# Summing the decays of both parities on TensorE for the first two token pairs, with a new order of all steps

## The chip, the cores and the metric

The kernel runs on one core of a Trainium2 chip. A core has five engines that run their own instruction streams: TensorE (PE, matrix products), VectorE (DVE), ScalarE (ACT), GpSimd (POOL) and SyncE (SP, which here only issues transfers), and sixteen DMA engines that carry transfers between the chip's memory (HBM) and the core's on-chip memory (SBUF). Matrix products end in a second on-chip memory, PSUM, with 8 banks. The metric is the device time of one execution in microseconds (us); lower is better. A median over several runs is compared.

## The reference

Two parts follow each other. The first is a linear attention with a gated state; its output is reshaped to tokens and goes through a two-layer network with the activation h * cos(h).

```python
batch, n_heads, seq, head_dim = (4, 8, 768, 48)
f = 1.0 / (1.0 + np.exp(-f_logit))
for t in range(S):
    state = f[:, :, t, :, None] * state + np.einsum('bhd,bhe->bhde', k[:, :, t], v[:, :, t])
    y[:, :, t] = np.einsum('bhd,bhde->bhe', q[:, :, t], state)
...
x = y.transpose(0, 2, 1, 3).reshape(B * S, H * D)       # 3072 x 384
h = x @ w_in                                            # 3072 x 2048
g = h * np.cos(h)
out = g @ w_out                                         # 3072 x 384
```

All inputs and the output are float32.

## The kernel before

**Tiling.** The 3072 tokens are cut into 12 *pairs* of 256 tokens (three pairs to a batch element). A pair has 128 partitions with two neighbouring tokens each, the even and the odd *parity* (`e` in the code), and in time two halves `g` of 128 tokens. All 8 heads are handled together, in two groups `u` of 4. The network works on the same 256-token units: its first layer is cut into 8 steps per unit (`h0.00` is unit 0, column quarter 0, half 0: 6 matmuls of 256 columns), its second into 8 (`o2.3` is output tile 2 of 128 tokens, quarter 3 of the hidden columns: 4 matmuls of 384 columns).

**The steps of a pair**, by name: the gate's logits, k, q and v are loaded (`f`, `k`, `q`, `v`, transfers issued on SP; pairs 0 and 1, in the list `HALVES`, load f, k and q in two halves, so `q0.1` is pair 0, heads 4 to 7). ACT makes log(1 + exp(-f)) (`ex`, `ln`). The decay over time is a running sum of this, made on PE by a product with a triangular matrix (`cum`), and ACT takes the exponential of it with both signs (`eb`, `ei`). q is multiplied by the one and k by the other (`qm`, `km`). Before, the sum is common to both parities of a partition, and the step by which they differ is put in ahead: `fx` (ACT) recovers a gate, `qa` multiplies q of the even parity, `ka` k of the even parity. q and k are turned, for pairs 0 to 3 by PE (`tq`, `tk`, copied from PSUM by `qkt`), from pair 4 on by a transposing transfer on SP (`tq`). PE makes the scores (`sc`), DVE masks them (`am`), PE multiplies them with v (`y`; v is converted by `vb` and rearranged by four `vt`), and PE adds the part of the state carried in (`yi`). The output goes to SBUF by two `xe`. The state is k times v (`ps`, PE); DVE adds the old state (`st`) and multiplies by the total decay (`sz`).

**The network**: `w0.i` and `w1.i` load the two weights in four blocks each, and `wc` converts them. After two `h` steps ACT takes the cosine (`co`) and DVE multiplies (`g`). After four `o` steps the tile is copied from PSUM (`ot`) and sent out (`out`).

**The order.** Nothing is scheduled at run time. A string, `ORDER`, lists every step with its engine's letter (T is PE, S ACT, V DVE, G POOL, Y SP) and the buffers that it takes; `emit` walks it, and each engine runs its own steps in that order, waiting by semaphores where data or a buffer is not there yet. So a step that waits holds up all that stands behind it on its engine. `SLOTS` gives the number of buffers of each kind. Steps `zf` are matmuls of zeros (`ZEROS` of them) that nothing reads; they stand on PE between the steps of the start. Steps `z..` with another name fill buffers with zeros once.

The profile names steps by line: `f`, `k`, `q`, `v` L296, `w` L282, `cum` L374 and L380, `eb` and `ei` L391 (pairs 0 and 1) and L395, `qa` L338 and L341, `ka` L351, `ad` (the sum of both parities for later pairs) L363, `qm` and `km` L404, `tq` and `tk` on PE L435 and as transfers L424, `sc` L456, `am` L461, `ps` L479, `st` L497, `sz` L503, `y` and `yi` L531, `g` L561, `h` L579, `co` L584, `o` L595, `out` L606, `zf` L264; all copies and conversions (`qkt`, `vb`, `vt`, `xe`, `ot`, `wc`) stand in one helper, L197, and are told apart by their tiles.

Of the kernel before, what the change touches and what calls it, by code (L numbers as in the profile page):

```python
# [16 lines left out]
C = 128  # L17
# [9 lines left out]
VHALVES = ()  # L27
TURN_QK = range(4, 12)
UNITS = [256] * 12
SLOTS = {"f": 3, "k": 3, "q": 3, "v": 3, "sp": 3, "ls": 2, "b": 3, "bi": 3, "qk": 3, "vb": 3, "vt": 3, "qkt": 5, "am": 4,  # L30
         "sz": 4, "x": 4, "g": 5, "co": 4, "ot": 4}
WITHIN = 12
ZEROS = 52
# [3 lines left out]
zvt.2:V zsp.2:V f0.1:Y0 zqk.2:G zsp.0:G f0.0:S ex0.1:S ln0.1:S2 f1.0:Y2 ex0.0:S fx0.1:S ln0.0:S  # L37
zf0:T0 zf1:T0 zf2:T0 zf3:T0 zf4:T0 zf5:T0 zf6:T0 zf7:T0 zf8:T0 zf9:T0 zf10:T0 cum0.0:T4 zvt.1:G
fx0.0:S zqk.0:G zsz.2:G k0.1:Y2 ka0.1:G cum0.1:T7 ei0.1:S1 km0.1:G0 eb0.0:S1 ei0.0:S ex1.0:S eb0.1:S
q0.0:Y0 v0:Y0 vb0:S0 ln1.0:S2 qa0.0:V qm0.0:V zsz.3:G zf11:T0 zf12:T0 zf13:T0 zf14:T0 zf15:T0  # L40
zf16:T0 zf17:T0 zf18:T0 zf19:T0 zf20:T0 zf21:T0 zf22:T0 zf23:T0 zf24:T0 cum1.0:T1 k0.0:Y ka0.0:G
km0.0:V zf25:T0 ps0.0:T6,7 f1.1:Y ex1.1:S ps0.1:T q0.1:Y ei1.0:S0 eb1.0:S0 ln1.1:S fx1.1:S qa0.1:V
sz0.01:V2 sz0.00:V st0.11:V f2:Y1 vt0.1:G2 zvt.0:V st0.10:V vt0.3:G qm0.1:G tk0.0:T0 tq0.0:T
qkt0.0:V0 v1:Y2 vt0.0:G ex2:S ln2:S1 k1.0:Y1 fx1.0:S zsp.1:G k1.1:Y zf26:T2 tk0.1:T6 zf27:T2 tq0.1:T
cum1.1:T3 qkt0.1:V1 zsz.1:G zsz.0:G zf28:T2 sc0.0:T4 am0.0:V2 sc0.1:T0 ad2:G0 sz0.10:V0 am0.1:V0
ei1.1:S eb1.1:S vb1:S1 vt1.2:S0 zf29:T2 zf30:T2 zf31:T2 zf32:T2 cum2:T2 ei2:S2 eb2:S2 ka1.0:V
zqk.1:G km1.0:V1 zf33:T6 zf34:T6 zf35:T6 zf36:T6 zf37:T6 zf38:T6 zf39:T6 zf40:T6 tk1.0:T4 ps1.0:T6,1
f3:Y0 ex3:S q1.0:Y1 sz0.11:V qa1.0:V q1.1:Y qa1.1:V qm1.1:V ln3:S0 fx3:S ka1.1:G vt0.2:G km1.1:G
ps1.1:T y0:T3,5 yi0:T xe0.0:S0 vt1.3:S vt1.1:S fy3:S st1.01:V st1.00:V sz1.01:V1 zf41:T0 zf42:T0
zf43:T0 tq1.1:T0 sz1.00:V qm1.0:G tq1.0:T qkt1.0:S2 tk1.1:T qkt1.1:V0 zf44:T2 zf45:T2 zf46:T2  # L50
zf47:T2 sc1.1:T6 xe0.1:V fx2:S ad3:G1 cum3:T0 ei3:S1 sc1.0:T4 am1.1:V1 am1.0:V3 w0.1:Y0 vt1.0:G
wc0.1:G zf48:T2 zf49:T2 zf50:T2 zf51:T2 h0.11:T2 h0.10:T yi1:T7,6 st1.11:V sz1.11:V3 y1:T xe1.1:V2
st1.10:V sz1.10:V eb3:S1 co0.1:S3 xe1.0:S g0.1:V3 fy2:S w0.0:Y1 wc0.0:G h0.01:T4 h0.00:T h1.01:T6
co0.0:S0 g0.0:V h1.00:T co1.0:S1 g1.0:V2 h1.10:T0 h1.11:T co1.1:S2 g1.1:V k3:Y2 ka3:G km3.1:G2
w0.3:Y4 wc0.3:G h0.31:T2 h0.30:T w0.2:Y0 wc0.2:G h1.21:T4 h1.20:T h0.20:T6 co0.3:S3 g0.3:V co1.2:S0
# [48 lines left out]
h9.00:T0 sz10.00:V1 st10.01:V sz10.01:V st10.11:V st10.10:V sz10.10:V0 sz10.11:V st11.00:V h9.01:T
co9.0:S3 st11.01:V g9.0:V1 h9.20:T4 h9.21:T h9.10:T2 co9.2:S0 sz11.01:V3 g9.2:V sz11.00:V o16.3:T6
# [83 lines left out]
def describe(nc, cpool, ppool, q, k, v, f_logit, moe_w_in, moe_w_out, out):  # L189
# [3 lines left out]
    def tl(shape, dt, name):  # L193
        return cpool.tile(shape, dt, name=name)
# [523 lines left out]
```

## Time and profile before

| | us |
|---|---|
| three runs | 180.91, 181.43, 182.29 |
| median | 181.43 |
| span of the profiled execution (first to last instruction) | 179.3 |
| median less that span | 2.13 |
| PE busy in the span | 171.0 (95%) |
| DVE, ACT, POOL busy | 137.8, 131.3, 109.2 |
| idle time of PE after 25 us, before matmuls | 1.2 |
| first `h` matmul | 25.1 |
| matmuls of zeros: 50 recorded | 14.8 |

The profiled execution is given by its span alone; the runs' times hold also what lies around a span. The profile's rows name a group by its source line, engine, operation and tiles, then count, busy time, mean of one in ns, and the idle time of the engine just before these instructions with what ended it. A time line's rows are start, duration, engine, line, operation. In the chain of waits each row is start, length and what the end was waiting for.

### The profile page before, as it was taken

The numbers are of one execution on the slowest core, as the hardware profiler recorded it, in microseconds if no ns is written. First come the engines' busy times: TensorE is split into PE (matmuls) and PEld (weight loads), VectorE is DVE, ScalarE is ACT, GpSimd is POOL, SyncE is SP. The second block draws the span as 40 slices with busy tenths as digits, with TensorE's granted clock in tenths as the row PEclk, the third lists the DMA queues.
The fourth block names the chain that finished last, engine by engine and source line by source line (L and its number), as shares of the span: only waits on it lengthen the run. The fifth ranks groups of instructions, "written<-read, shape, count | busy, mean of one in ns | idle before, by whom it ended". The sixth has DMA issues, their size and how long they took to land.

```text
span 179.3 us, 5727 instructions
## 1 busy us (share of the span) xinstructions
PE 171.0 (95%) x2412; PEld 122.9 (69%) x2414; DVE 137.8 (77%) x206; ACT 131.3 (73%) x185; POOL 109.2 (61%) x139
## 2 busy tenths in 40 slices
PE   7998899999999999999999998999999999999992
PEld 2453568876578866778668885668877766867761
DVE  6379998998894989969899887768689996385330
ACT  3899878886999998988999979858973702364410
POOL 7498699976979998789977295827992000000000
PEclk9999999999999999999999999999999999999999
DMA  6999999999999799999999999959045900004013
GB/s 156 262 261 287 356 324 315 306 274 328 257 257 236 168 190 180 282 277 198 249 203 262 226 254 207 234 131 268 4 106 121 148 0 4 4 0 176 0 50 129
DMA packets 74394, 34.46 MB, mean 192 GB/s; under 512 B 67456, under 2 KB 72832, under 8 KB 74368
## 3 DMA queue, kind: packets, MB, share of 16 engines
q1 hardware_dynamic: 73696, 33.79, 81.4%
q8 instruction: 19, 0.31, 0.8%
q10 hardware_dynamic: 672, 0.30, 0.6%
q14 instruction: 7, 0.06, 0.1%
HBM read 25.17 MB, written 4.72 MB: 167 GB/s over the span
## 4 chain that ended last, share of the span: by engine, by line
PE 69%; DMA 10%; POOL 7%; SPq 5%; DVE 5%; issue 3%; ACT 0%; POOLq 0%; DVEq 0%; ACTq 0%
PE ps L595 29%; PE ps L579 29%; DMA q<-in_q_dram 7%; SPq L296 5%; PE ps L531 4%; DMA qkt<-qk 3%; PE ps L456 3%; POOL qk L404 3%; PE ps L479 1%; POOL sp L363 1%; PE ps L435 1%; DVE qk L404 1%; POOL vt L197 1%; DVE sz L503 1%; PE ps L374 1%
## 5 line engine op out<-in xcount | busy, mean ns | idle before, releaser
L561 DVE TENSOR_TENSOR g<-ps,co 128x1024 bf16<-128x1024 f32 x48 | 57.7, 1221 | 15.3 <-ACT co L584 11.3
L595 PE MATMUL ps<-w_out_bf,g 128*128 128x384 bf16 x384 | 68.4, 326 | 0.0
L579 PE MATMUL ps<-x,w_in_bf 128*128 128x256 bf16 x576 | 66.7, 273 | 0.4 <-issue 0.4
L584 ACT ACTIVATE co<-ps,halfpi 128x1024 bf16<-128x1024 f32 x48 | 52.6, 1115 | 17.7 <-PE ps L579 14.4
L579 PEld LDWEIGHTS <-w_in_bf 128*128 128x128 bf16 x576 | 55.8, 98 | 9.2 <-issue 0.6
L595 PEld LDWEIGHTS <-g 128*128 128x128 bf16 x384 | 36.0, 98 | 21.5
L461 DVE TENSOR_TENSOR am<-ps,pmask 128x1024 bf16<-128x1024 f32 x24 | 28.7, 1215 | 3.6 <-PE ps L456 3.5
L404 POOL TENSOR_TENSOR qk<-q,b 128x384 bf16<-128x384 f32 x22 | 21.9, 1002 | 2.6 <-DVE q L338 1.7
L404 POOL TENSOR_TENSOR qk<-k,bi 128x384 bf16<-128x384 f32 x22 | 21.9, 1007 | 1.6 <-ACT bi L391 1.1
L197 POOL COPY vt<-vb 64x384 bf16<-64x384 bf16 x31 | 15.9, 514 | 1.4
L264 PE MATMUL ps<-zero 128*128 128x512 bf16 x50 | 14.8, 435 | 1.3 <-DVE zero L203 1.2
L503 DVE TENSOR_TENSOR sz<-ps,b 64x192 bf16<-64x192 f32 x40 | 14.2, 354 | 1.9 <-PE ps L479 0.9
L351 POOL TENSOR_TENSOR k<-k,f 128x384 f32<-128x384 f32 (+1 forms) x13 | 11.7, 904 | 6.2 <-DMA k<-in_k_dram 2.9
L197 DVE COPY ot<-ps 128x384 f32<-128x384 f32 (+1 forms) x17 | 8.7, 519 | 8.5 <-PE ps L595 6.0
L341 POOL TENSOR_TENSOR q<-f,q 128x384 f32<-128x384 f32 x10 | 10.0, 999 | 8.1 <-DMA q<-in_q_dram 8.1
L363 POOL TENSOR_TENSOR sp<-ls 128x384 bf16<-128x384 f32 x10 | 10.3, 1029 | 4.4 <-issue 2.2
L497 DVE TENSOR_TENSOR ps<-ps,sz 64x192 f32<-64x192 f32 x32 | 11.7, 366 | 1.4 <-PE ps L479 0.3
L329 ACT ACTIVATE f<-f 128x768 f32<-128x768 f32 (+1 forms) x14 | 10.4, 748 | 2.7 <-DMA f<-in_f_logit_dram 2.5
L197 ACT CAST x<-ps 128x384 bf16<-128x384 f32 x12 | 5.5, 479 | 8.6 <-PE ps L531 8.6
L197 ACT COPY ot<-ps 128x384 f32<-128x384 f32 (+1 forms) x9 | 4.1, 455 | 8.9 <-PE ps L595 8.9
L456 PE MATMUL ps<-qkt 48*64 48x128 bf16 (+1 forms) x320 | 8.6, 219 | 1.9 <-DVE qkt L197 1.0
L264 PEld LDWEIGHTS <-zero 128*128 128x128 bf16 x52 | 5.1, 108 | 6.9 <-issue 2.5
(61 smaller groups left out, 166.2 us busy)
## 6 DMA issues: line engine op xcount, KB each, us to landing
v<-in_v_dram SPq DMA_DIRECT2D x12, 384.0 KB, 6.1
out_dram<-ot SPq DMA_DIRECT2D x22, 192.0 KB, 2.8
f<-in_f_logit_dram SPq DMA_DIRECT2D x10, 384.0 KB, 5.6
k<-in_k_dram SPq DMA_DIRECT2D x10, 384.0 KB, 6.1
q<-in_q_dram SPq DMA_DIRECT2D x10, 384.0 KB, 6.4
g<-in_moe_w_in_dram SPq DMA_DIRECT2D x4, 768.0 KB, 7.5
g<-in_moe_w_out_dram SPq DMA_DIRECT2D x4, 768.0 KB, 7.2
k<-in_k_dram SPq DMA_DIRECT2D x4, 192.0 KB, 5.0
```

Source lines behind the costliest of these rows:

```text
L197: (nc.scalar.copy if e == "ACT" else eng(e).tensor_copy)(out=o, in_=i)
L264: G.step(f"zf{i}", ("PE",), lambda e, dump=dump: nc.tensor.matmul(dump.ap, lhsT=zero[:, 0:128], rhs=zero, start=True, stop=True), writes=[ ...
L351: eng(e).tensor_mul(out=w.ap[:, :, 0, :], in0=w.ap[:, :, 0, :], in1=t.ap[:, :, 0, :])
L363: G.step(f"ad{n}", ("POOL",), lambda e: eng(e).tensor_add(out=sp.ap[:, 0, :, 0:D], in0=soft.ap[:, :, 0, :], in1=soft.ap[:, :, 1, :]), read ...
L404: G.step(f"{nm}{n}.{u}", ("POOL", "DVE") if cut else ("POOL",), lambda e, u=u, j=j, src=src, dec=dec: eng(e).tensor_mul(out=qkp[u][j].ap[: ...
L456: nc.tensor.matmul(o[t0:t1, r, 2 * a + g, :].rearrange("p (e n) -> p e n", e=2), lhsT=wide[s, t0 // 64, :] if turned else wide[s].rearrang ...
L461: G.step(f"am{n}.{u}", ("DVE",), lambda e, u=u, sc=sc: nc.vector.tensor_mul(out=am[u].ap.rearrange("p r b n -> p (r b) n"), in0=sc.ap.rear ...
L503: eng(e).tensor_mul(out=new.ap[s, :, r, :].rearrange("p (u a) n -> p u a n", u=2), in0=view()[s].rearrange("p (u a) n -> p u a n", u=2), i ...
L561: nc.vector.tensor_mul(out=o.rearrange("p b (n e) -> p b n e", e=2), in0=ph.ap.rearrange("p (b e n) -> p b n e", e=2, n=64), in1=co.ap.rea ...
L579: nc.tensor.matmul(ph.ap[:, i * T:(i + 1) * T].rearrange("p (g t) -> p g t", t=C), lhsT=w_in_bf[:, kk, f0:f0 + 128], rhs=xa[:, :, kk, :], ...
L584: G.step(f"co{m}.{j}", ("ACT",), lambda e, ph=ph, co=co: nc.scalar.activation(out=co.ap, in_=ph.ap, func=AF.Sin, bias=halfpi), reads=[ph], ...
L595: nc.tensor.matmul(po.ap[:, 0:DM], lhsT=gT.ap[:, j, i * C:(i + 1) * C], rhs=w_out_bf[:, j, :], start=(po.first and j == 4 * s), stop=(po.f ...
```

## The change

For pairs 0 and 1 the running sum is now made for each parity by itself. `cum` does four matmuls of 192 columns for a half in the place of two: for the odd parity's contribution to the even one it takes the strict triangle. So the steps `fx`, `qa` and `ka` of these pairs are left out, and `eb` and `ei` are twice as wide (388 and 384 columns for 196 and 192) into new buffers `bb`, `bj`. For pair 1 (`CARRY_PE`) the old state is no longer added by DVE: `si` multiplies it with the identity on PE and sums it into the same PSUM bank. There are 33 matmuls of zeros for 52. `VLIE` and what belongs to it is empty and adds no instruction. The order of all steps is new.

```diff
-ZEROS = 52
+VLIE = ()
+CARRY_PE = (1,)
+ZEROS = 33
...
         pcs = [Val(p1), Val(p1)] if cut else [Val(p1)]
         xe = (0, 1) if cut else (0,)
+        W = HB * len(xe)
 
         def cum(e, o, h0, hn):
...
-            for x in xe:
-                nc.tensor.matmul(o[:, :, 0:HB], lhsT=incl,
-                                 rhs=w[:, x, :, 0:D].rearrange("p (u h) d -> p u h d", u=un),
-                                 start=(x == 0), stop=False)
+            for z in xe:
+                for x in xe:
+                    nc.tensor.matmul(o[:, :, HB * z:HB * z + HB], lhsT=strict if x > z and cut else incl,
+                                     rhs=w[:, x, :, 0:D].rearrange("p (u h) d -> p u h d", u=un),
+                                     start=(z == 0 and x == 0), stop=False)
...
-        for nm, dst, dh, sc, w in (("eb", bt, bth, -1.0, HB + 4), ("ei", bi, bih, 1.0, HB)):
+        for nm, dst, dh, sc, w in (("eb", bt, bth, -1.0, W + 4), ("ei", bi, bih, 1.0, W)):
...
             G.step(f"ln{n}{u}", ("ACT",), lambda e, t=t, s=s: ln(e, t, s), reads=[t], writes=[s], table="E")
+            if cut:
+                continue
...
-            if S0 is not None:
+            if S0 is not None and n in CARRY_PE:
+                def add(e, g=g, S0=S0):
+                    for r in range(2):
+                        nc.tensor.matmul(ps[g].ap[:, 0:HB].rearrange("p (a n) -> p a n", n=D), lhsT=ident,
+                                         rhs=S0.ap[:, :, r, :], start=(ps[g].first and r == 0),
+                                         stop=(ps[g].final and r == 1))
+                G.step(f"si{n}.{g}", ("PE",), add, reads=[S0] + both, writes=[ps[g]], sums=True)
+            elif S0 is not None:
...
-zvt.2:V zsp.2:V f0.1:Y0 zqk.2:G zsp.0:G f0.0:S ex0.1:S ln0.1:S2 f1.0:Y2 ex0.0:S fx0.1:S ln0.0:S
+f0.0:Y1 zf0:T7 f0.1:Y zf1:T2 f1.1:Y2 zsz.0:G v0:Y0 k0.1:Y0 k1.0:Y1 ex0.0:S q0.1:Y0 zsp.2:V zsz.2:V
```

The first place is the start of the program. SP's queue of loads before (f, k, q and v are the inputs, the number behind a name is the buffer):

```order
L296 DMA f_94<-in_f_logit_dram 128x4x96
L296 DMA f_96<-in_f_logit_dram 128x4x96
L296 DMA k_99<-in_k_dram 128x4x96
L296 DMA q_100<-in_q_dram 128x4x96
L296 DMA v_103<-in_v_dram 128x8x96
L296 DMA k_99<-in_k_dram 128x4x96
L296 DMA f_96<-in_f_logit_dram 128x4x96
L296 DMA q_100<-in_q_dram 128x4x96
```

And now:

```order
L309 DMA f_96<-in_f_logit_dram 128x4x96 x2
L309 DMA f_97<-in_f_logit_dram 128x4x96
L309 DMA v_104<-in_v_dram 128x8x96
L309 DMA k_98<-in_k_dram 128x4x96
L309 DMA k_99<-in_k_dram 128x4x96
L309 DMA q_101<-in_q_dram 128x4x96
L309 DMA f_97<-in_f_logit_dram 128x4x96
L309 DMA k_98<-in_k_dram 128x4x96
L309 DMA q_103<-in_q_dram 128x4x96
L309 DMA q_101<-in_q_dram 128x4x96
```

One more half of f, which ACT issued before, is in SP's queue, and the last row, `q0.0`, moved from the fourth place of SP's queue to the eleventh; halves of pair 1 (`k_99`, `f_97`, `q_103`) went ahead of it.

DVE in the same stretch before, from the masks of pair 0's scores (`am`) on; `k` and `q` rows are `ka` and `qa`, `qk` rows `km` and `qm`, `ps<-ps,sz` is `st`:

```order
L461 TENSOR_TENSOR am_131<-ps_158,pmask 128x1024
L351 TENSOR_TENSOR k_98<-k_98,f_96 128x4x48
L404 TENSOR_TENSOR qk_118<-k_98,bi_114 128x8x48
L503 TENSOR_TENSOR sz_135<-ps_161,b_112 64x4x48
L338 SCALAR_TENSOR_TENSOR q_101<-f_96,q_101 128x4x48 x2
L404 TENSOR_TENSOR qk_118<-q_101,b_111 128x8x48
L497 TENSOR_TENSOR ps_161<-ps_161,sz_135 64x192 x2
L503 TENSOR_TENSOR sz_136<-ps_161,b_111 64x4x48 x2
```

And now, from the same `am` on:

```order
L494 TENSOR_TENSOR am_137<-ps_165,pmask 128x1024
L544 TENSOR_TENSOR sz_141<-ps_166,bb_124 64x4x48 x2
L196 CAST x_147<-ps_166 128x384
L544 TENSOR_TENSOR sz_143<-ps_164,bb_124 64x4x48
L196 COPY qkt_133<-ps_163 128x1024
```

Between the masks of pair 0 and the state of pair 1, DVE has lost the preparation of k and q and the additions of the old state.

POOL in the same stretch now, from `vb1` to the first converted weight block (`wc0.1`) and the two `vt` steps behind it:

```order
L196 CAST vb_122<-v_105 128x768
L416 TENSOR_TENSOR qk_120<-k_99,bj_126 128x8x48
L416 TENSOR_TENSOR qk_120<-q_103,bb_124 128x8x48
L416 TENSOR_TENSOR qk_120<-k_99,bj_126 128x8x48
L196 COPY vt_130<-vb_121 64x8x48
L241 MEMSET sz_141 128x384
L373 TENSOR_TENSOR sp_108<-ls_110 128x8x48
L241 MEMSET qk_118 128x32x16
L416 TENSOR_TENSOR qk_120<-q_103,bb_124 128x8x48
L373 TENSOR_TENSOR sp_109<-ls_110 128x8x48
L196 CAST w_in_bf<-g_151 128x3x512
L196 COPY vt_128<-vb_122 64x8x48 x2
```

All four multiplies of pair 1 stand on POOL here, with the conversion of its v; before, POOL had two of the four.

The second place is the end of the program on ACT, the last copies and outputs, before:

```order
L584 ACTIVATE co_151<-ps_161,halfpi 128x1024
L197 COPY ot_154<-ps_158 128x384
L197 COPY ot_155<-ps_158 128x384
L197 COPY ot_152<-ps_160 128x192
L606 DMA out_dram<-ot_152 128x192
```

And now:

```order
L639 ACTIVATE co_153<-ps_164,halfpi 128x1024
L196 COPY ot_158<-ps_166 128x192
L661 DMA out_dram<-ot_158 128x192 x2
L661 DMA out_dram<-ot_159 128x192
L196 COPY ot_159<-ps_166 128x192
L661 DMA out_dram<-ot_159 128x192
L196 COPY ot_160<-ps_165 128x384
L196 COPY ot_158<-ps_165 128x384
```

The halved tiles 22 and 23 are no longer the last: the last two copies are whole tiles (20 and 21), and SP sends them; four issues of halves moved to ACT's queue.

More of the change, by code (lines that the diff above doesn't have):

```diff
@@ L38 @@
[L38 to L55, printed above, removed]
@@ new lines @@
+zf15:T6 zsp.1:G tk0.0:T5 ei1.1:S0 zf16:T4 qm0.0:V q1.1:Y tq0.0:T cum1.0:T6 qkt0.0:S0 w0.1:Y3
+ps0.0:T0,7 vb1:G1 zf17:T1 zf18:T1 ei1.0:S ps0.1:T zf19:T3 eb1.0:S sz0.00:V0 w0.0:Y1 km1.0:G2
+sz0.01:V zf20:T6 ex2:S zf21:T6 st0.11:V zf22:T5 qm1.0:G qkt0.1:V1 sc0.0:T0 ln2:S0 ps1.0:T6,3
+sz0.11:V2 sc0.1:T4 km1.1:G zf23:T2 st0.10:V vt1.1:S0 zf24:T2 am0.0:V2 zf25:T2 w0.2:Y2 fx2:S zf26:T2
+vt0.0:G tq1.0:T2 vt1.3:S ps1.1:T zsz.1:G sz0.10:V zf27:T0 ad2:G1 am0.1:V1 tk1.0:T si1.0:T k3:Y1
+zf28:T1 ex3:S zf29:T0 zqk.0:G zf30:T0 yi0:T7 sz1.01:V1 qm1.1:G ln3:S0 y0:T5 sz1.00:V si1.1:T
```

229 lines of the change are left out of this document (140 added, 89 removed).

## The prediction

> **What bounds the kernel now.** I read the page's first table first.
>
> ```profile
> PE 171.0 (95%) x2412; PEld 122.9 (69%) x2414; DVE 137.8 (77%) x206; ACT 131.3 (73%) x185; POOL 109.2 (61%) x139
> ```
>
> TensorE (PE) is the engine to follow, but 95% is an average over stages with different limits. So I took the groups of PE from 25 us to the end, with the idle time before them, and then the chain of waits.
>
> ```profile
> L579 PE MATMUL ps<-x,w_in_bf 128*128 128x256 bf16 x576 | 66.7, 273 | 0.4 <-issue 0.4
> L456 PE MATMUL ps<-qkt 48*64 48x128 bf16 (+1 forms) x288 | 7.0, 219 | 0.8 <-DMA qkt<-qk 0.6 <-ACT bi L395 0.2
> ```
>
> After 25 us PE is idle for 1.2 us in all (0.4 + 0.8). Time can come only from three places: the start before the first real MoE matmul, that 1.2 us, and the tail. The chain of waits shows start and end (start us, us, what):
>
> ```profile
> 6.01 4.53 DMA q<-in_q_dram
> ...
> 16.84 1.08 DVE k L351
> ...
> 19.66 1.17 DVE qk L404
> ...
> 25.08 1.31 PE ps L579 x12
> 26.39 0.90 PE ps L531 x56
> 27.29 2.73 PE ps L579 x24
> ...
> 168.21 7.81 PE ps L595 x48
> ```
>
> The start hangs on a load of q until 10.5 us and then on VectorE (DVE), which prepares pairs 0 and 1. First `h` at 25.08; two `h` steps and pair 1's output are done at 27.29; from there PE is packed to 168.21 + 7.81 = 176.02. The span is 179.3 us, the median of the runs 181.43, so 2.13 us lie outside the span; I add changes to that median.
>
> **Start.** The change takes off DVE, for pairs 0 and 1, four `qa`, one `ka`, two `km` and the four `st` of pair 1:
>
> ```profile
> L338 DVE SCALAR_TENSOR_TENSOR q<-f,q 128x192 f32<-128x192 f32 x4 | 1.4, 363 | 2.6 <-DMA q<-in_q_dram 2.6
> L497 DVE TENSOR_TENSOR ps<-ps,sz 64x192 f32<-64x192 f32 x32 | 11.7, 366 | 1.4 <-PE ps L479 0.3
> ```
>
> 4 x 0.363 + 4 x 0.366 + the 1.08 us of `ka` in the chain are 4.0 us even without `km`, so the old DVE chain is gone. What is late next? First the loads. Rows of POOL and DVE that waited for loads:
>
> ```profile
> 6.01 0.59 POOL L351 TENSOR_TENSOR k<-k,f 128x192 f32<-128x192 f32 x1 [2.07 <-DMA k<-in_k_dram]
> 10.56 0.38 DVE L338 SCALAR_TENSOR_TENSOR q<-f,q 128x192 f32<-128x192 f32 x1 [0.20 <-DMA q<-in_q_dram]
> ```
>
> In units of a 192 KB half load, k0.1 was the 4th on the queues and q0.1 the 10th: 6 units in 4.55 us, 0.76 us each. In the new order q0.0 is the 12th unit (it was the 5th): 6.01 + 8 x 0.76 = 12.1 us. The first w_in block is unit 21 to 24 in both: about 21.2 us. That `f0.0` moves from ACT's queue to the head of SyncE's (SP) I cost at nothing: ACT's first work waits for the data, and the count starts with the same three f halves. Now the pieces behind q0.0 (groups: busy, mean ns; then one row of PE's time line):
>
> ```profile
> L404 DVE TENSOR_TENSOR qk<-q,b 128x384 bf16<-128x384 f32 x2 | 2.5, 1234 | 0.7 <-ACT b L391 0.6
> L197 ACT COPY qkt<-ps 128x1024 bf16<-128x1024 bf16 x2 | 2.0, 1002 | 0.5 <-PE ps L435 0.5
> L395 ACT ACTIVATE bi<-ps 128x384 f32<-128x384 f32 x10 | 4.7, 489 | 1.5 <-PE ps L380 1.5
> L461 DVE TENSOR_TENSOR am<-ps,pmask 128x1024 bf16<-128x1024 f32 x24 | 28.7, 1215 | 3.6 <-PE ps L456 3.5
> 12.50 0.39 PE L435 MATMUL ps<-ident,qk 128*128 128x128 bf16 x4
> ```
>
> `qm0.0` on DVE ends at 12.1 + 1.23 = 13.3, `tq0.0` on PE at 13.7, `qkt0.0` on ScalarE (ACT) at 14.7. `cum1.0` is queued on PE behind `tq0.0` and hides under that copy: the nearest row is the transposes' 0.39 us for four matmuls, and eight give 0.8; if it took over 1.0, the rest would shift by the excess. `ei1.0`, now as wide as the L395 row, ends at 15.2 and releases GpSimd (POOL). POOL then has, without a gap: `km1.0`, `qm1.0`, `km1.1`, `vt0.0`, a memset, `ad2`, a memset, `qm1.1`, `ad3`, `wc0.1`, and `vt1.2`, `vt1.0`, `wc0.0`.
>
> ```profile
> L404 POOL TENSOR_TENSOR qk<-k,bi 128x384 bf16<-128x384 f32 x22 | 21.9, 1007 | 1.6 <-ACT bi L391 1.1
> L404 POOL TENSOR_TENSOR qk<-q,b 128x384 bf16<-128x384 f32 x22 | 21.9, 1002 | 2.6 <-DVE q L338 1.7
> L363 POOL TENSOR_TENSOR sp<-ls 128x384 bf16<-128x384 f32 x10 | 10.3, 1029 | 4.4 <-issue 2.2
> L197 POOL COPY vt<-vb 64x384 bf16<-64x384 bf16 x31 | 15.9, 514 | 1.4
> L197 POOL CAST w_in_bf<-g 128x1536 bf16<-128x1536 f32 x4 | 5.8, 1464 | 0.3 <-DMA g<-in_moe_w_in_dram 0.3
> L231 POOL MEMSET sz<- 128x384 bf16 x4 | 1.6, 421 | 0.0
> L231 POOL MEMSET qk<- 128x512 bf16 x3 | 1.6, 540 | 0.0
> ```
>
> To the end of `wc0.1`: 3.02 + 0.51 + 0.42 + 1.03 + 0.54 + 1.00 + 1.03 + 1.46 = 9.0, so 24.2 us; then 1.03 + 1.46, so `wc0.0` ends at 26.7. DVE arrives together with it: `qm1.1` ends on POOL at 21.7, its transposes (0.4), one state product before and one after, and the copy bring DVE to about 23.6, and two `am` (2 x 1.215) to 26.1; `y1` follows by 26.6. So PE stands at 26.7 where it stood at 27.29: 0.6 us gained. Of ACT's removed `fx` and its wider `eb` and `ei` only `qkt0.0` and `ei1.0` stand on this path, and they are in the sum. The wait added is that of the two `si` steps for pair 0's state: queued behind `si1.0` on PE are `yi0` and `y0`, and `y0` waits longer anyway, for `am0.1` on DVE. I cost `si` at nothing; without that cover each is two 192-column matmuls, together under 0.4 us by the transposes' row. Bounds: the best start has `wc0.1` right behind its load, 21.2 + 1.46 = 22.7 for the first `h` against 25.08, a gain of 2.4; the worst stretches POOL as in these rows of the two engines:
>
> ```profile
> 16.53 1.17 POOL L404 TENSOR_TENSOR qk<-k,bi 128x384 bf16<-128x384 f32 x1
> 20.38 1.31 POOL L363 TENSOR_TENSOR sp<-ls 128x384 bf16<-128x384 f32 x1
> 16.76 1.15 DVE L351 TENSOR_TENSOR k<-k,f 128x192 f32<-128x192 f32 x1
> ```
>
> 1.17 against 1.007 and 1.31 against 1.029, 16 to 27% on 11.5 us, 1.8 to 3.1 us lost, so at worst 2.5 slower. I take the undisturbed means, since both long POOL rows lie beside DVE instructions that read two SBUF tiles (the L351 row, and the L404 row at 19.66 in the chain), and in the new order DVE has none of these after 13.3 us. [...]
>
> **Fillers.** 52 become 33. One, `zf32`, now stands behind the first `h`:
>
> ```profile
> 1.19 4.88 PE L264 MATMUL ps<-zero 128*128 128x512 bf16 x11 [1.19 <-DVE zero L203]
> 7.09 3.21 PE L264 MATMUL ps<-zero 128*128 128x512 bf16 x14
> ```
>
> It costs 3.21 / 14 = 0.23 us. The others lay before 25.08 where PE waited anyway.
>
> **Middle.** The same `h`, `o` and attention steps in another order: no PE work more or less. I keep 1.2 us of stalls; bounds 0 (a gain of 1.2) and the rival below.
>
> **Tail.** The last two outputs now are whole 192 KB tiles: `ot21` on ACT, `out21` on SyncE's queue. Before, it was two half copies and halves of 96 KB.
>
> ```profile
> 176.79 0.35 ACTq L606 DMA_DIRECT2D out_dram<-ot  x1
> L197 ACT COPY ot<-ps 128x384 f32<-128x384 f32 (+1 forms) x9 | 4.1, 455 | 8.9 <-PE ps L595 8.9
> out_dram<-ot SPq DMA_DIRECT2D x7, 192.0 KB, 2.1
> out_dram<-ot ACTq DMA_DIRECT2D x1, 96.0 KB, 1.6
> v<-in_v_dram SPq DMA_DIRECT2D x12, 384.0 KB, 6.1
> ```
>
> Before: 0.77 + 1.6 = 2.37 us from the last matmul to landing. Now 0.05 + 0.46 + 0.03 + 2.1 = 2.64: 0.3 us more. Ahead of the two copies ACT now has two half copies and four output issues, four times 0.35 by the first row: counted from the end of `o22.2`, 3.25 us before the end, they take 2 x 0.46 + 4 x 0.35 = 2.3 us and are through 0.3 us before tile 20's last matmul; without that cover the tail grows by what is over. Bounds: 0 if ACT is at hand at once, and 1 us if `out20`, issued 0.65 us earlier, delays it (twice the size in one queue; the v row, 6.1 us among other loads, is the far bound and no neighbour here).
>
> Sum: -0.6 + 0.23 + 0 + 0.3 = -0.1, so 181.3 us. 1% (1.8 us) is about what measurement can tell from no change.
>
> **Rivals.** *Faster*: the loads land sooner than by count, POOL starts early, and the start wins its bound of 2.4: 181.43 - 2.4 + 0.23 + 0.3 = 179.6, or 178.8 with the 0.8 us of L456 stalls gone. For it: DVE was the chain, and 4 us leave it. Against: the two `km` and `vb1` that leave DVE and ACT go to POOL, which loses only three half-size `ka` for them.
>
> *Slower, by pair 9*: three score steps `sc9.0`, `sc8.0`, `sc8.1` now stand together behind 60 `h` and 49 `o`; before, `sc9` came behind 54 `o`.
>
> ```profile
> 102.13 1.00 POOL L341 TENSOR_TENSOR q<-f,q 128x384 f32<-128x384 f32 x1 [4.53 <-DMA q<-in_q_dram]
> 105.76 5.91 DMA qkt<-qk
> 118.55 0.64 PE L456 MATMUL ps<-qkt 48*64 48x128 bf16 x32
> ```
>
> Without five `o` (7.81 / 12 = 0.65 each), two `cum` and pair 8's scores before it, PE reaches `sc9.0` about 6 us before 118.55, near 112.5. A transpose took 5.91 us from issue, so `qm9.0` must end on POOL by 106.6. If k9 and q9 land at 102.1 as q did, the eight POOL instructions from there (8 us) end at 110, the tile lands at 116, and PE stalls 3.4 us less the old 0.6: 181.3 + 2.8 = 184.1. It decides from a landing later than about 98.5. Against: q9 is now issued ahead of pair 7's transposes.
>
> *Slower, by the clock*: the first fillers took 4.88 / 11 = 0.44 us, later ones 0.23: PE ran at half speed for about 5.9 us after its first matmul. With two fillers before `cum0.0`, PE works steadily only from about 5 us. If PE falls back to that pace when `h` starts, 5.9 us at half pace lose 2.9: 184.2. Against: from `ps0.0` to the first `h` I count 15 fillers and half the transposes, with gaps of about 1 us, and before the change a gap like this did no harm:
>
> ```profile
> 18.65 0.38 PE L435 MATMUL ps<-ident,qk 128*128 128x128 bf16 x4 [0.93 <-DVE qk L404]
> ```
> [...]
>
> **How the numbers follow.** Forecast 0.57, its own range 180.0 to 182.8 (start and tail half way to their bounds); faster rival 0.20; pair 9 0.17; clock 0.06. Predicted 181.3. Range 179.0 to 184.1: it leaves out the best corner of the faster rival and the worst of POOL's stretch. Faster by over 1%: 0.20; within: 0.56; slower: 0.17 + 0.06 + 0.01 = 0.24.
>
> **What would show it.** Right: first `h` near 24.2, the second pair of `h` near 26.7, POOL without idle time from 15.2 to 26.7, q0.0 landing near 12.1, last `out` landing 2.6 us after the last matmul, PE idle after 25 us about 1.2. Wrong: a first `h` before 23 or after 25.5, PE waiting over 2 us for a transpose at `sc9.0`, or `h` matmuls at twice 0.11 us.

## The result, and the profile after

The changed kernel took 184.95 us (median of 4 runs, 184.13 to 185.57), and the kernel before 181.86 beside it on the same chip (4 runs, 180.91 to 183.27): a ratio of 1.0155 with an interval of 1.011 to 1.02. It is slower by about 3 us; 181.3 was predicted, with a range of 179.0 to 184.1. The profiled execution has a span of 183.2 us against 179.3. Medians here and below are over all runs, while ratios and their intervals leave out runs more than 1.5% above the fastest of their kernel, as about one in seven of the kernel before was, most of these with a mean clock near 0.99.

The start came out as it was worked out. From the time line of TensorE (PE) after, the first `h` steps (start us, duration, engine, line, operation):

```profile
23.88 1.49 PE L634 MATMUL ps<-x,w_in_bf 128*128 128x256 bf16 x12
...
26.44 4.76 PE L634 MATMUL ps<-x,w_in_bf 128*128 128x256 bf16 x42
```

The second pair of `h` steps stands at 26.44, against 27.29 before: 0.85 us gained. So the loss is later. The waits of PE from 25 us to the end (line waited for, total, times, longest):

```profile
PE ps L472 <- DMA qkt<-qk: 3.2, 2, 2.7
```

Before, PE had idled 1.2 us in the same stretch in all. Now scores wait 3.2 us for transposed q and k, 2.7 of it in one piece. The time line of PE around that piece:

```profile
67.26 0.42 PE L472 MATMUL ps<-qkt 48*64 48x128 bf16 x16 [0.49 <-DMA qkt<-qk]
...
72.16 0.42 PE L472 MATMUL ps<-qkt 48*64 48x128 bf16 x16 [2.73 <-DMA qkt<-qk]
72.51 0.90 PE L650 MATMUL ps<-w_out_bf,g 128*128 128x384 bf16 x4
...
73.67 1.44 PE L650 MATMUL ps<-w_out_bf,g 128*128 128x384 bf16 x4
...
76.91 0.81 PE L650 MATMUL ps<-w_out_bf,g 128*128 128x384 bf16 x4
```

The step that waits at 72.16 is `sc5.1`, the scores of pair 5. Behind it the same four `o` matmuls take 1.44 us where 3 us later they take 0.81. The busy time in stretches of 2 us, whose third column from the right is the granted clock of PE, says why:

```profile
72.00:74.00 2.00, 1.84 (x27) 1.12 (x28) 1.37 (x2) 0.55 (x2) 1.30 (x3) 0.78 0.79 140
74.00:76.00 2.00, 2.00 (x44) 1.21 (x46) 1.20 (x4) 1.11 (x3) 1.71 (x3) 0.50 1.13 308
76.00:78.00 2.00, 2.00 (x42) 1.46 (x35) 1.14 (x3) 1.38 (x4) 1.97 (x3) 0.87 1.24 276
```

The clock fell to 0.50 and came back (0.78, 0.50, 0.87). The shares that are missing in the three stretches of 2 us make (0.22 + 0.50 + 0.13) x 2 = 1.7 us of full-speed work lost, which is 3.4 us at half pace. And the chain of waits shows what `sc5.1` waited for:

```profile
66.03 6.08 DMA qkt<-qk
```

The transposing transfer `tq5.1` was issued at 66.03 and landed 6.1 us later. On the queue of SyncE (SP), before and then after:

```profile
59.71 2.71 SPq L424 DMA_TRANSPOSE qkt<-qk  x2
62.51 0.56 SPq L606 DMA_DIRECT2D out_dram<-ot  x1
63.18 1.31 SPq L424 DMA_TRANSPOSE qkt<-qk  x1
```

```profile
58.93 2.53 SPq L440 DMA_TRANSPOSE qkt<-qk  x1
61.56 0.52 SPq L661 DMA_DIRECT2D out_dram<-ot  x1
62.18 0.38 SPq L309 DMA_DIRECT2D f<-in_f_logit_dram  x1
62.65 2.19 SPq L440 DMA_TRANSPOSE qkt<-qk  x1
64.89 0.57 SPq L661 DMA_DIRECT2D out_dram<-ot  x1
65.55 0.39 SPq L309 DMA_DIRECT2D f<-in_f_logit_dram  x1
66.03 2.30 SPq L440 DMA_TRANSPOSE qkt<-qk  x1
```

`tq5.1` went out at 63.18 before and at 66.03 now, 2.85 us later: `out2`, `f7`, `out1` and `f9` stand between the three transposes now, `out0` alone did before, and the issue of one transpose takes 2.2 to 2.5 us, not 1.3 to 1.4. From 58.93 on SP has nearly no pause. The queue isn't all of it: `qm5.1`, which makes the data, ends on POOL at 64.78 now and at about 62.6 before.

The transfer also landed more slowly. For it alone, before and then after, the trace gives the length of its issue (ns) and the time from issue to landing (us):

```profile
L424 SPq DMA_TRANSPOSE qkt<-qk x1: 1311/1311/1311, 63.2 to 63.2; - x1
...
DMA to landing us min/median/max: 3.3/3.3/3.3
```

```profile
L440 SPq DMA_TRANSPOSE qkt<-qk x1: 2297/2297/2297, 66.0 to 66.0; - x1
...
DMA to landing us min/median/max: 6.1/6.1/6.1
```

So before it landed at 66.5, some 2 us ahead of its use:

```profile
68.61 0.39 PE L456 MATMUL ps<-qkt 48*64 48x128 bf16 x14
```

Now it lands at 72.1. Of the 5.6 us between, half is the later issue and half (6.1 against 3.3) the slower landing.

The account of the profiled spans: start -0.85, filler +0.23, waits of PE +2.0 (3.2 against 1.2), clock +1.7, and +0.23 at the end (3.51 us from the end of the last matmul to the end of the span, against 3.28). That is +3.3 of the +3.9; 0.6 us I can't place.

### The profile page after: what moved, and what is told of

Same layout as the page of the kernel before. It is cut to its first block, busy times and chain, and to the rows that moved or that the text cites. A ratio compares the mean times of both kernels' runs of the same rounds, so it can differ in the third digit from the quotient of the medians.

```text
span 183.2 us, 5686 instructions
## 1 busy us (share of the span) xinstructions
PE 170.8 (93%) x2407; PEld 122.8 (67%) x2407; DVE 128.6 (70%) x194; ACT 133.1 (73%) x187; POOL 107.8 (59%) x133
## 4 chain that ended last, share of the span: by engine, by line
PE 57%; DMA 14%; POOL 13%; SPq 9%; issue 3%; ACTq 1%; ACT 0%; DVE 0%; POOLq 0%
PE ps L650 25%; PE ps L634 24%; DMA k<-in_k_dram 11%; SPq L309 9%; POOL qk L416 7%; PE ps L572 4%; DMA qkt<-qk 3%; PE ps L472 2%; POOL k L360 2%; POOL q L350 2%; PE ps L512 1%; ACTq L661 1%; POOL w_in_bf L196 1%; POOL w_out_bf L196 1%; PE ps L386 1%
## 5 line engine op out<-in xcount | busy, mean ns | idle before, releaser
L650 PE MATMUL ps<-w_out_bf,g 128*128 128x384 bf16 x384 | 68.6, 328 | 0.1
L416 POOL TENSOR_TENSOR qk<-k,bi 128x384 bf16<-128x384 f32 x20 | 19.8, 998 | 0.8 <-ACT bi L407 0.2
L416 POOL TENSOR_TENSOR qk<-q,b 128x384 bf16<-128x384 f32 x20 | 19.8, 999 | 0.6
L196 POOL COPY vt<-vb 64x384 bf16<-64x384 bf16 x29 | 14.9, 514 | 8.4 <-ACT vb L196 6.1
L544 DVE TENSOR_TENSOR sz<-ps,b 64x192 bf16<-64x192 f32 x32 | 11.2, 353 | 2.1 <-PE ps L512 1.4
L196 ACT COPY ot<-ps 128x384 f32<-128x384 f32 (+1 forms) x14 | 6.1, 454 | 8.8 <-DVE ot L196 4.8
L277 PE MATMUL ps<-zero 128*128 128x512 bf16 x33 | 11.1, 431 | 1.5 <-DVE zero L202 1.2
L538 DVE TENSOR_TENSOR ps<-ps,sz 64x192 f32<-64x192 f32 x28 | 10.2, 366 | 2.8 <-PE ps L512 1.9
L472 PEld LDWEIGHTS <-qkt 48*64 48x64 bf16 (+1 forms) x320 | 5.9, 104 | 7.3 <-DMA qkt<-qk 3.7
L360 POOL TENSOR_TENSOR k<-k,f 128x384 f32<-128x384 f32 x10 | 9.9, 998 | 1.1 <-DMA k<-in_k_dram 0.6
L196 ACT COPY vt<-vb 64x384 bf16<-64x384 bf16 x19 | 9.6, 508 | 0.3
```

The source lines that it names most:

```text
L196: (nc.scalar.copy if e == "ACT" else eng(e).tensor_copy)(out=o, in_=i)
L360: eng(e).tensor_mul(out=w.ap[:, :, 0, :], in0=w.ap[:, :, 0, :], in1=t.ap[:, :, 0, :])
L416: G.step(f"{nm}{n}.{u}", ("POOL", "DVE") if cut else ("POOL",), lambda e, u=u, j=j, src=src, dec=dec: eng(e).tensor_mul(out=qkp[u][j].ap[: ...
L472: nc.tensor.matmul(o[t0:t1, r, 2 * a + g, :].rearrange("p (e n) -> p e n", e=2), lhsT=wide[s, t0 // 64, :] if turned else wide[s].rearrang ...
L544: eng(e).tensor_mul(out=new.ap[s, :, r, :].rearrange("p (u a) n -> p u a n", u=2), in0=view()[s].rearrange("p (u a) n -> p u a n", u=2), i ...
L650: nc.tensor.matmul(po.ap[:, 0:DM], lhsT=gT.ap[:, j, i * C:(i + 1) * C], rhs=w_out_bf[:, j, :], start=(po.first and j == 4 * s), stop=(po.f ...
```

## The experiments

All runs stand beside runs of the kernel before on the same chip (medians of 182.35 to 182.74 us). A line of a diff is a step in the order table, with its engine's letter (T PE, V VectorE, S ScalarE, G GpSimd, Y SP).

**Fill the wait.** `fill_wait` gives PE twelve matmuls of zeros where it waited.

```diff
-ZEROS = 33
+ZEROS = 45
...
 ad7:G2
+zf33:T0
...
+zf44:T0
 sc5.1:T0
```

> The changed kernel with 12 more matmuls of zeros on PE (ZEROS 45), placed right ahead of sc5.1, where PE waited 2.73 us for a transpose; nothing else moves. Theory 1 (the loss in the middle is the late transpose of pair 5 plus PE's clock, which fell to half for some 4 us after that wait): the twelve, at 0.215 us, fill 2.6 us of the wait, the granted clock stays at 1.0, the wait itself is still there: 1.9 to 2.3 us less than the changed kernel, about 182.8. Rival (the clock costs nothing, because PE is waiting for others there anyway): same as the changed kernel, 184.9, within 0.5.

Measured: 182.98 us (182.59 to 183.85, 10 runs), ratio 1.0029 (0.9994 to 1.0065). From the time line of PE and the stretch in which the clock had been 0.50:

```profile
69.00 2.76 PE L278 MATMUL ps<-zero 128*128 128x512 bf16 x11
71.70 0.42 PE L473 MATMUL ps<-qkt 48*64 48x128 bf16 x16
```

```profile
74.00:76.00 2.00, 2.00 (x65) 1.48 (x52) 1.87 (x6) 1.90 (x6) 1.34 (x3) 1.00 1.17 305
```

`sc5.1` starts 0.46 us earlier than in the changed kernel, PE has done nothing more that is of use, and most of the loss is gone. The granted clock is 1.00 in that stretch, where it had been 0.50. So here the idling cost more than the time it lasted: the clock is a cause of its own.

**Half of the filling.** `fill_six` has six of these matmuls in the same place (`zf33` to `zf38`, `ZEROS = 39`).

> Edit: the changed kernel with six idle matmuls (of the kind of its fillers, zeros into a free bank) right ahead of sc5.1, half of those of the run fill_wait, where eleven in the trace took 2.76 us. They end at about 70.4, so the wait for the transpose is cut from 2.7 to some 1.3 us, and its end doesn't move. Theory (the clock falls with the length of the unbroken wait; at 1.96 us it fell in some runs of pool_sp and not in others, so 1.3 is short enough): clock 0.997 or more in every run and 182.5 to 183.5, as fill_wait. Rival (any wait of this place brings it down): clock 0.98 to 0.99 and 184.2 to 185.5.

Measured: 182.76 us (181.47 to 185.61, 10 runs), ratio 1.0 (0.9963 to 1.0038); the clock was 0.997 or more in every run. In the profile the rest of the wait is 0.70 us, less than the expected 1.3, since the transpose landed earlier (70.79). So this run doesn't show what a gap of 1.3 does; the profile of `old_order`, below, holds one.

**The queue of SP.** `sp_first` puts three transfers behind the transpose.

```diff
 h3.11:T
-out2:Y
 vt4.1:G0
...
 qm5.1:G
-out1:Y
 o4.3:T
 g3.3:V
-f9:Y1
 km5.0:G
...
 tq5.1:Y4
+out2:Y
+out1:Y
+f9:Y1
 o4.2:T
```

> The changed kernel with three transfers on SP's queue (out2, out1, the load f9) moved from ahead of tq5.1 to behind it. Theory 1: tq4.0 and tq5.1 are issued earlier, tq5.1 at about 64.8 us (POOL's qm5.1 then sets it) for 66.03, so the wait at sc5.1 is about 1.5 us for 2.73 and the 0.49 at sc4.0 is gone: at least 1.5 us less than the changed kernel (183.4), and with a clock that no longer falls 3.5 less (181.5). Rival (the transposing transfers themselves are slow in this stretch because the DMA engines are full, whatever stands ahead in SP's queue): the landing moves by less than 0.5 us, and the time stays above 184.3.

Measured: 185.45 us (185.02 to 186.29, 4 runs), ratio 1.0153 (1.0055 to 1.0251). No gain, though `sc5.1` no longer waits: `tq5.1` is issued at 65.5, as soon as POOL has ended `qm5.1`, and lands 3.1 us later. Most of what it gained is landing (3.1 against 6.1 us), not issue (65.5 against 66.03). Another wait stands in its place, here in the time line of PE, and behind it in that of ScalarE (ACT):

```profile
74.90 0.51 PE L572 MATMUL ps<-qkt,sz 128*32 128x128 bf16 x12 [2.91 <-ACT ot L196]
```

```profile
72.82 0.84 ACT L342 ACTIVATE f<-f 128x768 f32<-128x768 f32 x1 [2.77 <-DMA f<-in_f_logit_dram]
73.57 0.92 ACT L356 ACTIVATE f<-ls 128x384 f32<-128x384 f32 x2
74.39 0.46 ACT L196 COPY ot<-ps 128x384 f32<-128x384 f32 x1
```

ACT's `ex9` waits for the load `f9` that I had moved. The copies `ot5` and `ot4` stand behind it in ACT's order and run at 74.39 and 75.14, and `ot5` holds the bank that the second half of `yi4` needs. The clock fell again (0.50 in the stretch from 76 to 78 us). A further wait of 0.69 us, at 32.41 us for a converted weight block, lies ahead of all that the edit moves.

**GpSimd too.** `pool_sp` adds a later place for three copies of GpSimd (POOL) that stood ahead of `qm5.1`.

```diff
-vb4:G0
...
-vt4.1:G0
...
-vt4.3:G
...
 qm5.1:G
+vb4:G0
+vt4.1:G0
+vt4.3:G
```

> As the run with the three SP transfers moved, and on POOL vb4, vt4.1 and vt4.3 moved from ahead of qm5.1 to behind it. Theory 1: qm5.1 ends about 62.2 us for 64.8, tq5.1 is issued at about 64.2 behind tq4.0, the wait at sc5.1 is under 1 us, the clock stays at 1.0: 181.0 to 181.6. If SP's queue and not POOL sets the transposes, the same time as the run with SP alone, within 0.5. Rival: above 184.

Measured: 184.2 us (182.44 to 185.18, 10 runs), ratio 1.0086 (1.0034 to 1.0139). The wait behind `ex9` is shorter:

```profile
73.10 0.35 PE L572 MATMUL ps<-qkt,sz 128*32 128x128 bf16 x12 [1.96 <-ACT ot L196]
```

The time misses the expected 181.0 to 181.6. The runs of this one kernel fell in two groups, and the mean clock tells them apart: 182.44, 182.52 and 182.99 us at 1.0, and 183.68 to 185.18 (seven runs, mean 184.55) at 0.991. The profile is of the first group: there a wait of 1.96 us brought no fall. The groups lie 1.9 us apart, about the price of one fall; the waits of the second group are not recorded, so that it fell there at the same wait is not shown.

**ScalarE's order.** `ex9_later` is `pool_sp` with `ex9` next to `ex8`, behind the cosines.

```diff
 tq5.0:Y1
 ad6:G1
 o5.1:T
-ex9:S
 sz4.01:V
...
 ex8:S
+ex9:S
```

> Edit: the kernel of the run pool_sp (two output stores and load f9 behind tq5.1 on SP's queue, vb4, vt4.1, vt4.3 behind qm5.1 on GpSimd), and ScalarE's first exponential of pair 9 (ex9, which had waited 2.5 us for f9 with the copies ot5 and ot4 behind it) is put next to ex8, past the two groups of cosines. Theory (the loss is only order: a wait of TensorE of some 2 us or more in pair 5, and the clock that falls behind it): nothing waits in 65 to 76 us, the clock stays at 1.00, and the time is that of the runs of pool_sp at clock 1.00 (182.44, 182.52, 182.99) less their wait of 2.0: 180.6, range 180.0 to 181.6. Rival (the wait always finds another place, because VectorE, GpSimd and ScalarE together are short of time in the middle of this order): a new wait of 1.5 us or more on TensorE between 66 and 90 us, and 182.5 to 184.5.

Measured: 181.0 us (180.03 to 181.62, 11 runs), ratio 0.9918 (0.9886 to 0.9951). The only wait of PE from 25 us on that the profile shows:

```profile
PE ps L472 <- DMA qkt<-qk: 0.2, 1, 0.2
```

The steps that had been in question now stand so, in the time line of PE:

```profile
69.02 0.40 PE L472 MATMUL ps<-qkt 48*64 48x128 bf16 x14
...
71.10 0.52 PE L572 MATMUL ps<-qkt,sz 128*32 128x128 bf16 x24
```

`sc5.1` ends at 69.42, not 72.58, and `yi4` runs whole at 71.10. Seven moves, of three transfers, three copies and one exponential, turn +1.55% into -0.8%, with every part of the new computation left in place. A second set of runs, `ex9_again`, gave less:

> The kernel of the run ex9_later again, unchanged, on another occasion and beside the run old_tail. Theory: 0.986 to 0.997 of before once more, clock 1.00.

Measured: 181.01 us (180.37 to 182.31, 12 runs), ratio 0.9956 (0.9929 to 0.9983).

**Without GpSimd's moves.** `sp_ex9` is `sp_first` with the move of `ex9`.

> Edit: the kernel of the run sp_first (two output stores and load f9 behind tq5.1 on SP's queue) with ex9 moved next to ex8 on ScalarE; GpSimd's order stays that of the changed kernel. It tells whether the three moves on GpSimd are needed for the gain of ex9_later. Theory (SP's queue and ex9 are the loss; GpSimd's three copies only ahead of the waits by some tenths): no wait over 1 us on TensorE between 60 and 90 us, clock 1.00, 180.5 to 182.0. Rival (GpSimd's lateness still makes the transposes late): a wait of sc5.1 of 1 to 2 us, 182 to 184.

Measured: 183.37 us (181.32 to 184.19, 10 runs), ratio 1.0 (0.9946 to 1.0055), the clock 0.995 or more throughout. Again two groups: four runs at 181.32 to 181.71 and six at 183.3 to 184.19. The profiled execution, 184.04 us, is one of the six: PE waits 1.69 us for a product of POOL and 1.10 for a transpose in it, and the granted clock stays at 1.00 behind both. That is one execution; four runs reach the times of `ex9_later` and six don't, and why is open.

**The computation in the old order.** `old_order` has the new sums and identity products, but before's order around them: the table of before less the steps that are gone.

```diff
-fx0.1:S
...
-qa0.0:V
...
-ka0.0:G
...
 yi0:T
+si1.0:T
...
-st1.01:V
...
+si1.1:T
 h0.11:T2
```

> The new computation in the old order: pairs 0 and 1 sum both parities on PE, pair 1 carries its state by identity products, but the order is that of the kernel before, without the steps fx, qa, ka of pairs 0 and 1 and the four st of pair 1, with si1.0 behind yi0 and si1.1 ahead of the first h, and 52 matmuls of zeros. Theory 1 (the order of the middle costs, not the computation): no wait of over 1 us for a transpose, clock 1.0, first h at 25 us or up to 1 us earlier: 180.9 to 181.9. Rival (the wider sums and exponentials or the products on PE cost time): 183 or more.

Measured: 181.41 us (180.7 to 182.79, 10 runs), ratio 0.9955 (0.9913 to 0.9997). Its second pair of `h` steps and what follows:

```profile
26.42 5.85 PE L636 MATMUL ps<-x,w_in_bf 128*128 128x256 bf16 x52
```

That pair stands at 26.42, as with the new order (26.44). So the gain at the start comes with the computation, and the loss with the new order of the middle. In this profile PE also waits after 25 us, 2.8 us in three pieces, the longest 1.30 us (for a weight block) and 1.06 (for a transpose, just over the expected limit of 1). That is little less than the 3.2 us of the changed kernel, but the granted clock stays at 1.00 behind each: what sets the changed kernel apart is less the sum of its waits than the one long wait and the fall behind it.

**The wait put into the kernel before.** `late_tq` is the kernel before with one step moved.

```diff
-tq5.1:Y2
...
 f9:Y0
...
 tq5.0:Y3
...
 k6:Y2
+tq5.1:Y2
```

> Edit: the kernel before with one move, the transpose tq5.1 put behind f9, tq5.0 and k6 on SP's queue; no other instruction is moved. By the trace of before it is issued at about 66.0 instead of 63.2 us, lands some 6 us later at about 72, and sc5.1, which ran at about 68.5, waits some 3 us. Theory (a wait of TensorE near 3 us in the middle brings the clock down whatever the computation, and that costs about 2 us more): the wait of 2.5 to 3.5, the granted clock at 0.5 to 0.8 in some stretch behind it, mean clock about 0.99, and the time 4 to 6 us above before (ratio 1.022 to 1.033). Rival (the clock falls because of the new computation's own instructions, not the wait): clock 1.00 and 2.5 to 3.5 us above (1.014 to 1.019). Rival (before has the slack to take the wait in): below 1.008.

Measured: 186.07 us (185.76 to 186.54, 4 runs), ratio 1.0203 (1.016 to 1.0247), the clock 0.979 to 0.991. The wait in the time line of PE, then the stretches behind it:

```profile
72.92 0.64 PE L456 MATMUL ps<-qkt 48*64 48x128 bf16 x16 [3.25 <-DMA qkt<-qk]
```

```profile
72.00:74.00 2.00, 1.07 (x26) 0.86 (x27) 0.38 (x1) 0.00 (x0) 1.83 (x3) 0.67 1.24 286
74.00:76.00 2.00, 2.00 (x8) 0.99 (x7) 1.90 (x4) 0.00 (x0) 0.00 (x0) 0.50 1.20 298
76.00:78.00 2.00, 2.00 (x84) 1.55 (x82) 0.95 (x4) 1.38 (x4) 0.00 (x0) 0.97 1.28 261
```

The clock falls with none of the new computation: (0.33 + 0.50 + 0.03) x 2 = 1.7 us once more, of which 0.1 lies in the end of the wait. The time was below the 4 to 6 us expected, because I had added the new wait to the 1.2 us of old ones; the waits of this run are 3.5 in all. 3.5 - 1.2 + 1.7 = 4.0, measured 3.7.

**The two loads.** `loads_later` takes the loads `q6` and `v7`, which the change has ahead of the transposes, behind them, with what follows on `v7`'s buffer.

```diff
-q6:Y0
...
-v7:Y0
...
-vb7:G1
...
 tq5.0:Y1
+q6:Y0
+v7:Y0
...
-v6:Y0
...
+vb7:G1
+v6:Y0
 km6.1:G2
```

> Edit: the changed kernel with only the loads q6 and v7, which it has ahead of pair 4's and 5's transposes on SP's queue and which before has behind them, put back behind tq5.0 (the cast vb7 and load v6, which follow on v7's buffer, go with them). The stores and f9 stay where the change has them. Theory (half of the lateness of tq5.1, 2.85 us against before, is the two more loads in the queue: GpSimd gets v4 0.8 us late from them, and each transpose's issue takes 2.2 to 2.5 us behind full rings against 1.4): tq5.1 is issued by about 64.5, the wait of sc5.1 shrinks from 2.7 to 1.5 or less, the clock holds, and the time is 182.0 to 183.2. Rival (the two stores and two small loads between the transposes are all of it): tq5.1 is issued within 0.5 us of 66.0, the wait stays at 2.2 to 2.9, the clock falls, 184 to 185.5.

Measured: 190.56 us (190.09 to 191.16, 4 runs), ratio 1.0445 (1.039 to 1.05). The time is a miss by my edit: it made `v6` late, and `km6.0` stands behind the conversion of `v6` in POOL's order. From the waits of PE, its longest, and from the time line of POOL:

```profile
PE ps L512 <- POOL qk L416: 7.9, 1, 7.9
```

```profile
84.03 0.82 POOL L196 CAST vb<-v 128x768 bf16<-128x768 f32 x1 [5.65 <-DMA v<-in_v_dram]
```

But up to there the run answers its question. SP issued the transpose earlier, and PE went on sooner:

```profile
65.11 2.17 SPq L440 DMA_TRANSPOSE qkt<-qk  x1
```

```profile
69.78 0.42 PE L472 MATMUL ps<-qkt 48*64 48x128 bf16 x16 [0.61 <-DMA qkt<-qk]
```

That is 0.92 us earlier to issue (66.03 to 65.11) and 2.4 us earlier to run `sc5.1` (72.16 to 69.78): the landing itself is quicker without the two loads (4.7 us from issue to start of `sc5.1`, not 6.1). The wait left is 0.61, not 2.73. So the lateness is not that of the stores and small loads between the transposes alone. Without those, in `sp_first`, or without the two large loads ahead, here, most of the wait of `sc5.1` is gone; it took both. Why an issue takes 2.2 to 2.5 us in one order and 1.3 to 1.4 in the other no trace here shows; the full rings of the expectation were a guess of mine. In the wait of 7.94 us, which ends at 85.86, the clock had already fallen (0.73 from 82 to 84 us), and it was at 0.50 to 0.57 from 84 to 90 us.

**The end.** `old_tail` is `ex9_later` with tiles 20 and 21 finished ahead of 22 and 23, as before.

```diff
 g11.1:V
+g11.2:V
+o20.0:T
...
+ot21:S1
+ot20:S3
...
 o23.3:T6
-g11.2:V
...
+out23.1:Y
+ot23.0:V
 out23.0:S
-o21.3:T
-ot20:S3
-out20:Y
-ot21:S1
-out21:Y
```

> Edit: the kernel of ex9_later with the end of before: the last four products of tiles 20 and 21 ahead of those of 22 and 23, their stores on SP, and the two halves of 22 and 23 last. It tests the term of the tail by itself, which the prediction put at +0.3 us and the two profiles at 3.50 against 3.28 us from the end of the last matmul to the end of the span. Theory: 0.2 us less than ex9_again (0 to 0.4), that is 180.8 beside 181.0, and 3.2 to 3.35 us in the profile. Rival (the products of 20 and 21 had covered the last gelu product g11.2, or the stores of SP): a wait of TensorE for g11 of 0.3 us or more before the last products, and no gain or up to 0.5 us lost.

Measured: 180.86 us (180.12 to 181.99, 12 runs), ratio 0.9931 (0.9904 to 0.9958), beside 181.01 for `ex9_again`. The difference of 0.15 us is inside the spread of either, and from the last matmul to the end of the span it is 3.66 us against 3.79 in `ex9_again`: not the 3.2 to 3.35 expected. A gain of the end is not shown.

## Why the prediction was wrong

**Start: right.** q0.0 let VectorE start at 12.57, not 12.1, but `qm0.0` then took 0.56 us and not the 1.23 I had given it, so the two misses cancelled. POOL began `km1.0` at 15.16 and had no gap, with its products at 0.99 to 1.00 us each, the first `h` stood at 23.88 (24.2 was worked out), the second pair at 26.44 (26.7). The sum had -0.6 where -0.85 was measured.

**Fillers and tail: right as far as they can be seen.** The tail was put at +0.3 and its spans differ by +0.23; `old_tail` doesn't confirm it.

**Middle: the step that failed.** "The same `h`, `o` and attention steps in another order: no PE work more or less. I keep 1.2 us of stalls." The work of PE was the same, the stalls were not: 3.2 us in place of 1.2, since `tq5.1` was issued 2.85 us later and then took 2.8 us longer to land. I had compared the places of PE's steps at pair 9 alone, and nowhere else set SP's and POOL's order against PE's. The rows of before would have given the slack: `tq5.1` issued at 63.18 landed at 66.5, and `sc5.1` came at 68.6. The later issue alone would have used that up (a landing at 69.3, with PE there at 69.4 now); the slower landing made it a wait of 2.7 us. That the transfers newly ahead slow the landing, `sp_first` (3.1 us) and `loads_later` (4.6 us) show.

**The rival by pair 9** had the right mechanism, a late transpose, at the wrong place. At pair 9 PE doesn't wait. Its 184.1 lay near the measured time by luck: it counted 2.8 us of wait, where there were 2.0 more, and the clock made up the rest.

**The rival by the clock** had the right mechanism, the wrong place and too high a price. I looked for the fall at the first `h`, where the granted clock stayed at 1.00 (22 to 30 us), and priced it at 2.9 us (5.9 us at half pace; the granted clock reads 1.00 in that stretch of before, so the pace was read from the lengths of the matmuls alone). It came behind the wait of 2.73 us in the middle, held for 3.4 us and cost 1.7. What I missed is that the two rivals are one: behind a wait of 2.73 us in packed work the clock came down, so that wait cost 2.73 + 1.7 = 4.4 us. `fill_wait` (wait filled, clock 1.00) and `late_tq` (a wait of 3.25 us, clock 0.50) show it each in another way, and the two groups of `pool_sp` fit it. On the length of the gap the runs give single cases: the clock fell behind 2.73 us in the profile of the changed kernel, whose four runs all have a mean clock of 0.981 to 0.989, and stayed at 1.00 behind 1.96 us in the profile of `pool_sp`. Why the half pace lasts 3.4 us, in the after and `late_tq` profiles alike, no run here shows.

**The forecast's sign.** The computation is what I took it for: worth 0.5% in the old order (0.0 to 0.9). What I gave no number to was the order table, and it decided: +1.55% as changed, -0.8% and -0.4% in two sets of runs with those seven steps moved. That version is faster than both kernels, though by under 1% against the one before.

## What to carry to other kernels

Where an order is fixed by hand or by a search, compare for every transfer that the bound engine waits for when it lands and when it is used, and count the transfers and large loads that newly stand ahead of it: here its issue came 2.85 us later and its landing took 2.8 us longer, so a slack of 2 us was not enough. Price a new wait of the bound engine at its length plus what the clock loses behind it: 1.7 us here behind waits of 2.73 to 3.25 us, and nothing in the profiles whose longest waits are 1.30 and 1.96. Where a wait can't be removed, idle matmuls in it can take most of that second part away, as the twelve of `fill_wait` did (clock 1.00, ratio 1.0029 for 1.0155), and a move of one transfer has to be followed to the engine that consumes it and to the steps behind it there, as from `f9` to `ex9`, `ot5` and `ot4`.

## What the runs showed of the hardware that I had not expected

After 40 us of packed work a wait of 2.73 us was followed by a granted clock of 0.50, and the fall lost 1.70, 1.70 and 1.72 us in the three profiles with one (after, `sp_first`, `late_tq`). Read in stretches of 0.1 us, the half pace runs from 73.12 to 76.53, from 74.83 to 78.24 and from 72.70 to 76.11: 3.41 us each time, with waits of 2.73, 2.91 and 3.25 us. In `loads_later` it runs from 82.91 to 89.73, 6.82 us, and starts 2.95 us before the wait of 7.94 us ends. For `sp_first` these are the stretches:

```profile
74.00:76.00 2.00, 1.10 (x44) 1.09 (x43) 0.00 (x0) 2.00 (x7) 1.31 (x2) 0.71 1.06 265
76.00:78.00 2.00, 2.00 (x22) 0.96 (x12) 1.55 (x4) 1.54 (x5) 1.92 (x4) 0.50 1.15 321
78.00:80.00 2.00, 2.00 (x31) 1.50 (x30) 0.65 (x2) 1.00 (x1) 0.99 (x2) 0.94 1.26 268
```

The product `qm0.0` on VectorE, of the same size and types, took 1.23 us before (mean of two) and 0.56 after:

```profile
9.88 0.56 DVE L416 TENSOR_TENSOR qk<-q,bb 128x384 bf16<-128x384 f32 x1 [5.21 <-ACT bb L403]
12.57 0.56 DVE L416 TENSOR_TENSOR qk<-q,bb 128x384 bf16<-128x384 f32 x1 [2.13 <-DMA q<-in_q_dram]
```

Both start while POOL runs no such product, and before, each had run beside one (1.30 us at 7.85 with POOL's at 7.74, 1.17 us at 19.66 with POOL's at 19.36). So the mean in the group's row is that of products with such a neighbour, where I had used it as the price of the instruction. Before's own rows for the product of k on VectorE say the same: 0.56 us at 9.81 and at 17.94, where POOL has no product. No run moves one such product alone, so what makes them longer is not shown.
